# 128-key chunks with a shared tail, stacked scores and per-pair key sums in a fused attention and two-MLP kernel

## Chip, cores and metric

The kernel runs on one core of a Trainium2 chip. The metric is the device time of one execution in microseconds (us). Times of a whole execution are medians over runs. The trace is that of one profiled execution of the kernel before; its times count from the start of the span that the profiler recorded.

## What is computed

Soft-capped attention over 4 batches, 12 heads, 448 positions and 64 features per head, followed by two MLPs over the 1792 tokens (768 features, 2048 hidden).

```python
scores = (q @ k.T) / sqrt(64)
scores = cap * tanh(scores / cap)
attn = exp(scores - max) / (sum(exp(scores - max)) + 1e-09)
x = (attn @ v).transpose(0, 2, 1, 3).reshape(1792, 768)
h = relu(x @ w_in)
x = (h * h) @ moe_w_out
h = x @ moe2_w_in
out = (h / (1 + exp(-1.702 * h))) @ moe2_w_out
```

The weights of the MLPs come as 64-bit floats and are unpacked to 32 bits on the chip.

## The kernel before

With the cap of this input (30) only `bounded_cap` does work; the other version of the kernel, `any_cap`, stands in a branch that is not taken.

**Precision.** Most products are sums of rounded parts: an operand is split into `hi` (rounded to the fp32r type by ScalarE) and `lo` (the rest, by VectorE), and TensorE multiplies the parts and adds them up in PSUM. The attention of batches 0 and 1 (`PLAIN`) multiplies exp(scores) by V as plain fp32 instead; each such product appears as two matmul records. One matmul has 448 moving columns nearly everywhere.

**Attention.** Heads are worked in pairs, 6 pairs per batch; a pair's two heads lie in partitions 0 to 63 and 64 to 127 of the tiles of q and k. Scores are made transposed, keys on partitions: the 448 keys are cut into 4 chunks of 112 (`CP`, `NCH`). For one chunk `scores` issues 6 matmuls: three terms (hi·hi, hi·lo, lo·hi), each for both heads, with 64 rows of the array for each head. `tanhs` and `exps` (ScalarE) then work on 112 partitions and 2 x 448 columns, and `pv` multiplies by V for each head (in batches 2 and 3 once for the hi part of exp and once for the lo part). V's tile has 128 columns per head: in batches 0 and 1 the values and a block of ones, so that the sums over keys come out in the other half of the same matmul; in batches 2 and 3 the hi and the lo part of V.

**Sums of batches 2 and 3.** `add_keys` adds up the chunks of exp on VectorE, `sum_keys` multiplies the split result by a column of ones into 12 partitions of PSUM (one row for each head of the batch), and `take_sums` (VectorE) collects them. Only after the sixth pair of the batch `recip` takes the reciprocals, in four pieces of 112 columns, and splits them; `normalize` spreads them over partitions by matmuls against `spread` (2 for each pair, hi and lo) and multiplies. Batches 0 and 1 use `divide` for each pair instead: a reciprocal of `ct` [128 x 448] (in one piece in batch 0, in four pieces of 112 columns in batch 1), then the product.

**Order.** Work is issued in quarter slots T. Pair n of the 24 begins at `begin[n]` = 8n, plus 14 (`LATE`) from batch 1 on; `PREP`, `PLAN0` (batches 0 and 1) and `PLAN` (2 and 3) say which step goes at which slot after that. Batch 0 runs alone up to slot 52. Then come the four stages of the MLPs, one for each batch, with 68 weight units each; a unit is 15 or 18 matmuls (`product`), and behind each unit `attn` issues as many slots of the next batch's attention as `ready` asks for: in stage 1 (batch 1 in the MLPs, batch 2 in attention) 58 slots, in stage 2 48. A scheduler at build time orders the instructions of each engine from this. Engines take their instructions in order.

**Queues.** SyncE (SP) issues the loads of q, k, v and of the weights (`Q_LOAD`, `Q_V`), GpSimd (POOL) the stores of the first three stages (`Q_OUT`). q and k of batch 0 are transposed by TensorE (`kps`, `qps`), those of the later batches by VectorE.

Of the kernel before, what the change touches and what calls it, by code (L numbers as in the profile page):

```python
# [677 lines left out]
def bounded_cap(ctx, tc, q, k, v, cap, w1, w2, w3, w4, out):  # L678
# [26 lines left out]
    NCH = S // CP  # L705
# [7 lines left out]
    Q_KEEP = nc.sync  # L713

# [7 lines left out]
    LATE = 14  # L722
# [8 lines left out]
    OB = 2  # L731

# [31 lines left out]
    one = const.tile([P, 2 * P], F32R, name="one")  # L764

    spread = [const.tile([P, 2, D], F32R, name=f"spread{i}") for i in range(NP)]
    sums = const.tile([P, S], F32, name="sums")
    rcp = const.tile([P, 2, S], F32R, name="rcp")

    def emit_const():  # L770
        nc.sync.dma_start(out=capt, in_=cap.rearrange("(o n) -> o n", o=1).to_broadcast([P, 1]))
# [10 lines left out]
        nc.gpsimd.memset(f32(one[:, P - 1 : P]), 1.0)  # L782
        nc.gpsimd.memset(f32(rcp), 0.0)

    def emit_spread():
        for i, s in enumerate(spread):
            nc.vector.tensor_copy(s, ident[:, 2 * i : 2 * i + 2].unsqueeze(2).to_broadcast([P, 2, D]))
# [4 lines left out]

    def load_pair(b, p):
        if b in DVE_QK:

            qt = ld.tile([P, S // 32, 32], F32, tag="q", name="qt")
            kt = ld.tile([P, S // 32, 32], F32, tag="k", name="kt")
            for t, src in ((kt, k), (qt, q)):
                for j in range(4):
                    Q_LOAD.dma_start(  # L800
                        out=t[32 * j : 32 * j + 32],
                        in_=src[b, 2 * p + j // 2, :, 32 * (j % 2) : 32 * (j % 2) + 32].rearrange(
                            "(c p) d -> p c d", p=32
                        ),
                    )
        else:
            qt = ld.tile([CP, NCH, 2, D], F32, tag="q", name="qt")
            kt = ld.tile([CP, NCH, 2, D], F32, tag="k", name="kt")
            for t, src in ((kt, k), (qt, q)):
                for j in range(2):  # L810
                    Q_LOAD.dma_start(
                        out=t[:, :, j, :], in_=src[b, 2 * p + j].rearrange("(p c) d -> p c d", c=NCH)
                    )
        raw[b, p] = (qt, kt)

    def transposed(b, t, name):

        if b in DVE_QK:
            y = ld.tile([P, S], F32, tag="tt", name=name)
            nc.vector.transpose(y, t.rearrange("p c d -> p (c d)"))  # L820
            return y
        ps = ps_x.tile([P, 512], F32, tag="x" if name == "kps" else "z", name=name)
        for c in range(NCH):
            cols = slice(c, S, NCH) if name == "qps" else slice(c * CP, (c + 1) * CP)
            nc.tensor.transpose(ps[:, cols], t[:, c].rearrange("p h d -> p (h d)"), ident[:CP, :CP])  # L825
        return ps[:, :S]

    def load_v(b, p):
        if b in PLAIN:

            vt = vst[b, p] = v_p.tile([CP, NCH, 4, D], F32, tag="v", name="vt")
            nc.gpsimd.memset(vt[:, :, 1:3, :], 1.0)
            for j in range(2):
                Q_V.dma_start(
                    out=vt[:, :, 3 * j, :],
                    in_=v[b, 2 * p + j].rearrange(
                        "(c p) d -> p c d" if b in DVE_QK else "(p c) d -> p c d", c=NCH
                    ),
                )
            return  # L840
        vt = v_p.tile([CP, NCH, 2, D], F32, tag="vraw", name="vraw")
        for j in range(2):
            Q_V.dma_start(out=vt[:, :, j, :], in_=v[b, 2 * p + j].rearrange("(c p) d -> p c d", c=NCH))
        vst[b, p] = vt

    def split_v(b, p, half):

        if half == 0:
            t = vst[b, p]
            vs = v_p.tile([CP, NCH, 4, D], F32R, tag="v", name="vs")  # L850
            vst[b, p] = (t, vs)
            nc.scalar.activation(vs[:, :, 0::3, :], t, AF.Copy)
        else:
            t, vs = vst[b, p]
            nc.vector.tensor_tensor(vs[:, :, 1:3, :], t, f32(vs[:, :, 0::3, :]), ALU.subtract)
            vst[b, p] = vs

    def prep_k(b, p, step):
# [531 lines left out]
```

## Time and profile before

| what | us |
|---|---|
| median of 3 runs | 1204.43 |
| lowest, highest run | 1200.18, 1208.26 |
| profiled execution, its own time | 1205.74 |
| its span in the trace | 1203.9 |
| TensorE busy in the span | 1180.6 |
| VectorE busy | 782.1 |
| ScalarE busy | 746.0 |

The span is what lies between the first and the last recorded instruction. PE is TensorE's matmuls, PEld its weight loads, DVE VectorE, ACT ScalarE, POOL GpSimd, SPq the queue of SyncE. The granted TensorE clock is 1.00 of its full 2.4 GHz level in every stretch before the last. Matmuls overlap each other, so the duration of one matmul is not its cost; the distance from one start to the next is. The stages lie as follows: batch 0's attention alone from 0 to 82 us, MLPs of batch 0 with attention of batch 1 to about 390 us, MLPs of batch 1 with attention of batch 2 to about 676 us, then two more, and the last stage without attention.

### The profile page before, as it was taken

To read this page: it belongs to the slowest core of one execution; us is meant where nothing else is said; L and a number is where in the kernel's file an instruction comes from. 1 tells how busy PE (TensorE), PEld (TensorE's weight loads), DVE (VectorE), ACT (ScalarE), POOL (GpSimd) and SP (SyncE) were. 2 spreads that over 40 slices of the span, in tenths; PEclk is the share of its full clock that TensorE was granted. 3 is DMA by queue.
4 is the path that set the end of the run, shared out by engine and by line. 5 is a ranking of instruction groups with operands and counts; after the bars stand their busy time and mean duration, and the time that the engine had idled before them with its cause. 6 is when DMAs were issued, how large, how long until landed. Compare 5 with 4: busy or idle time off the path is not lost.

```text
span 1203.9 us, 15272 instructions
## 1 busy us (share of the span) xinstructions
PE 1180.6 (98%) x5688; PEld 993.8 (83%) x5688; DVE 782.1 (65%) x1078; ACT 746.0 (62%) x1071; POOL 54.5 (5%) x95
## 2 busy tenths in 40 slices
PE   7989999999999999999999999999999999999997
PEld 3448877777777888888888888888899999999996
DVE  2578476776769947787677965676646753564454
ACT  5989677877679647676667575666643444344431
POOL 1000000000001300000000400000000310000000
PEclk9999999999999999999999999999999999999999
DMA  4469877888787753443333432223323432333323
GB/s 107 104 175 321 247 223 233 258 269 230 223 242 240 211 141 93 115 121 102 90 112 108 123 115 78 96 70 105 101 71 118 136 121 94 116 114 111 100 98 50
DMA packets 193223, 174.03 MB, mean 145 GB/s; under 512 B 116466, under 2 KB 165618, under 8 KB 193138
## 3 DMA queue, kind: packets, MB, share of 16 engines
q1 hardware_dynamic: 185266, 168.13, 46.8%
q0 software_dynamic: 2304, 4.13, 1.7%
q10 hardware_dynamic: 5568, 0.69, 0.4%
q8 instruction: 47, 0.77, 0.3%
q14 instruction: 38, 0.31, 0.1%
HBM read 142.25 MB, written 30.67 MB: 144 GB/s over the span
## 4 chain that ended last, share of the span: by engine, by line
PE 92%; ACT 4%; DMA 2%; DVE 1%; issue 1%; SPq 0%; DVEq 0%; ACTq 0%
PE mps L1205 76%; PE vps L935 8%; PE sps L892 6%; DMA wraw<-in_moe_w_in_dram 1%; PE sums L983 1%; ACT e L903 1%; DMA keep<-y 1%; ACT ct L951 1%; ACT wh L1185 1%; ACT e L899 1%; ACT sx L1161 0%; PE rps L1016 0%; DVE y L1168 0%; PE qps L825 0%; DMA qt<-in_q_dram 0%
## 5 line engine op out<-in xcount | busy, mean ns | idle before, releaser
L1205 PE MATMUL mps<-xt,wh 128*128 128x448 f32 x1536 | 444.7, 371 | 4.1 <-ACT xt L1030 1.8
L1205 PE MATMUL mps<-g,wh 128*128 128x448 f32 x1536 | 443.7, 370 | 1.0 <-ACT wh L1185 0.6
L1185 ACT ACTIVATE wh<-wraw 128x768 fp32r<-128x768 f32 (+1 forms) x204 | 164.5, 807 | 275.1 <-PE mps L1205 261.4
L1205 PEld LDWEIGHTS mps<-xt,wh 128*128 128x128 f32 x1536 | 286.1, 188 | 41.3 <-issue 7.6
L1205 PEld LDWEIGHTS mps<-g,wh 128*128 128x128 f32 x1536 | 286.1, 188 | 38.0 <-ACT wh L1185 5.1
L1186 DVE TENSOR_TENSOR wl<-wraw,wh 128x768 fp32r<-128x768 f32 (+1 forms) x204 | 185.4, 909 | 175.0 <-ACT wh L1185 172.8
L1205 PE MATMUL mps<-g,wl 128*128 128x448 f32 x768 | 281.8, 367 | 1.0 <-DVE wl L1186 1.0
L1205 PE MATMUL mps<-xt,wl 128*128 128x448 f32 x768 | 281.4, 366 | 0.0
L1205 PEld LDWEIGHTS mps<-g,wl 128*128 128x128 f32 x768 | 144.3, 188 | 14.6 <-DVE wl L1186 1.9
L1205 PEld LDWEIGHTS mps<-xt,wl 128*128 128x128 f32 x768 | 144.3, 188 | 13.0 <-DVE wl L1186 0.4
L1234 ACT ACTIVATE g<-r 128x448 fp32r<-128x448 f32 x128 | 73.5, 574 | 62.3 <-DVE r L1230 33.2
L1235 DVE TENSOR_TENSOR g<-r,g 128x448 fp32r<-128x448 f32 x128 | 79.4, 621 | 45.4 <-ACT g L1234 44.8
L899 ACT ACTIVATE e<-sps 112x896 f32<-112x896 f32 x96 | 87.4, 911 | 23.0 <-PE sps L892 22.9
L903 ACT ACTIVATE e<-e,ecap 112x896 f32<-112x896 f32 x96 | 99.7, 1039 | 1.8
L1247 DVE SCALAR_TENSOR_TENSOR y<-mps,y 128x448 f32<-128x448 f32 x96 | 59.4, 619 | 57.4 <-PE mps L1205 56.8
L1186 DVE TENSOR_TENSOR wl<-y,wh 128x768 fp32r<-128x768 f32 (+1 forms) x68 | 61.9, 910 | 50.3 <-ACT wh L1185 49.5
L892 PE MATMUL sps<-qq,kk 64*112 64x448 f32 x576 | 90.0, 404 | 1.0 <-ACT qq L878 0.7
L935 PE MATMUL vps<-e,vt 112*128 112x448 f32 x192 | 85.9, 564 | 1.4 <-ACT e L903 0.4
L892 PEld LDWEIGHTS sps<-qq,kk 64*112 64x112 f32 x576 | 45.3, 175 | 46.5 <-issue 27.8
L1263 POOL DMA_DIRECT2D out_dram<-o x72 | 45.2, 635 | 648.5 <-DVE o L1261 648.0
L1161 ACT ACTIVATE sx<-wraw 128x768 f16<-128x768 bf16 (+1 forms) x68 | 69.4, 1021 | 7.0 <-DMA wraw<-in_moe_w_in_dram 5.8
L1168 DVE SCALAR_TENSOR_TENSOR y<-wraw,sx 128x768 int32<-128x768 int32 (+1 forms) x68 | 61.6, 906 | 10.3 <-ACT sx L1161 8.7
(74 smaller groups left out, 887.0 us busy)
## 6 DMA issues: line engine op xcount, KB each, us to landing
wraw<-keep SPq DMA_DIRECT2D x66, 768.0 KB, 4.3
wraw<-in_moe_w_in_dram SPq DMA_DIRECT2D x32, 766.5 KB, 6.4
wraw<-keep SPq DMA_DIRECT2D x36, 640.0 KB, 4.3
keep<-y SPq DMA_DIRECT2D x44, 384.0 KB, 3.4
wraw<-in_moe_w_out_dram SPq DMA_DIRECT2D x24, 638.8 KB, 5.8
wraw<-in_moe_w_out_dram SPq DMA_DIRECT2D x12, 766.5 KB, 6.6
keep<-y SPq DMA_DIRECT2D x24, 320.0 KB, 3.9
kt<-in_k_dram SPq DMA_DIRECT2D x72, 56.0 KB, 4.9
```

The costliest lines, as they stand in the source:

```text
L892: nc.tensor.matmul(ps[:CP, j, :S], kk[r, ik, c * CP : (c + 1) * CP], qq[r, iq, :], start=(i == 0), stop=(i == 2),)
L899: nc.scalar.activation(e, sc.pop((b, p, c))[:CP, :, :S], AF.Tanh)
L903: nc.scalar.activation(e, e, AF.Exp, scale=ecap[:CP])
L935: nc.tensor.matmul(pvp[b, p][j][:, :S], x, t[:, j, :], start=(c == 0 and n == 0), stop=(c == NCH - 1 and n == len(ts) - 1),)
L1161: pin(nc.scalar.activation(z, words(n, BF16)[:, :, :, 2], AF.Copy))
L1168: pin(nc.vector.scalar_tensor_tensor(y[:, :kn].bitcast(I32), words(n, I32)[:, :, :, 0], 13, sx[n % XZ][:, :kn], ALU.logical_shift_right, A ...
L1185: pin(nc.scalar.activation(hi[:, :kn], t[:, :kn], AF.Copy))
L1186: pin(nc.vector.tensor_tensor(lo[:, :kn], t[:, :kn], f32(hi[:, :kn]), ALU.subtract))
L1205: nc.tensor.matmul(ps[:, :S], a[:, kk, :], r, start=(kk == 0 and i == 0), stop=(kk == kn - 1 and i == 2),)
L1234: nc.scalar.activation(g[:, 0, :], r, AF.Copy)
L1235: nc.vector.tensor_tensor(g[:, 1, :], r, f32(g[:, 0, :]), ALU.subtract)
L1247: nc.vector.scalar_tensor_tensor(y, ps[:, :S], scale, y, ALU.mult, ALU.add)
```

## The change

- **Chunks.** In batches 0, 2 and 3 the 448 keys of a head are cut into 3 chunks of 128 and a rest of 64. The rests of the two heads of a pair share one chunk: k lies in a tile of 512 columns per pair (`kz`), head a's 448 keys in columns 64 to 511, head b's first 384 in columns 128 to 511 and its last 64 in columns 0 to 63, with zeros beside the tail's keys in the other head's rows. The tail's scores are then one product over 128 rows, and `tanhs`, `exps`, `split_hi` and `split_lo` work on 448 columns there instead of 896. In `pv` the tail is two products over 64 rows. Batch 1 (`NATURAL`) keeps chunks of 112.
- **Stacked scores in batches 2 and 3.** For each head the 128 rows of the array hold q's hi part and its lo part; k's hi part and lo part are held twice, once in each half of the partitions. A chunk is 4 matmuls over 128 rows (2 for each head) instead of 6 over 64. The copy into the other half is made by two DMAs for each pair from the POOL queue (`Q_DUP`, step 3 of `prep_k`, five slots ahead of the pair's first scores). The ACT and DVE steps of `prep_k` and `prep_q` become two instructions of 64 partitions each.
- **Sums per pair.** `sum_keys` writes each head's sums on 64 partitions; `take_sums` (now on ACT) copies them to `ct`, and batches 2 and 3 use `divide` for each pair, as batch 1 does. `recip`, `normalize`, `spread`, `sums` and `rcp` are gone.
- **Order.** Batches 2 and 3 begin 12 quarter slots later (26 instead of 14). `ready` of batches 2 and 3 becomes 6 slots later, so stage 1 has 64 slots instead of 58; stage 2 stays at 48.

```diff
-    NCH = S // CP
+    NCH = 4
+    TAIL = NCH - 1
+    KW = NCH * P
+    STACKED = (2, 3)
+    NATURAL = (1,)
...
+    Q_DUP = nc.gpsimd
...
-    LATE = 14
+    LATE = (0, 14, 26, 26)
...
+    kz = [const.tile([P, KW], F32, name=f"kz{i}") for i in range(2)]
...
+        nc.vector.memset(kz[0][:32], 0.0)
+        nc.gpsimd.memset(kz[1][:32], 0.0)
...
+            Q_LOAD.dma_start(out=kt[16:, :, 0, :], in_=ka)
+            Q_LOAD.dma_start(out=kt[32:, :, 1, :], in_=kb[:96])
+            Q_LOAD.dma_start(out=kt[:16, :, 1, :], in_=kb[96:])
+            Q_LOAD.dma_start(out=qt[:, :, 0, :], in_=qa)
+            Q_LOAD.dma_start(out=qt[:, :, 1, :], in_=qb)
...
+        Q_V.dma_start(out=ta, in_=va[64:].rearrange("(c p) d -> p c d", p=P))
+        Q_V.dma_start(out=tb, in_=vb[: TAIL * P].rearrange("(c p) d -> p c d", p=P))
+        Q_V.dma_start(out=ca, in_=va[:64])
+        Q_V.dma_start(out=cb, in_=vb[TAIL * P :])
...
+        elif stacked:
+            kk = prep[b, p][1]
+            for j, r, o in halves():
+                Q_DUP.dma_start(out=f32(kk[o, j]), in_=f32(kk[r, j]))
...
+        tail = c == TAIL and b not in NATURAL
...
+        if b in STACKED:
+            todo = [(0 if tail else j, kk[:, j, i, cols], qq[:, j, :]) for j in range(2) for i in range(2)]
+        elif tail:
+            todo = [(0, kk[:, ik, cols], qq[:, iq, :]) for ik, iq in ((0, 0), (0, 1), (1, 0))]
...
+    def chunk(b, c, t):
+        if b in NATURAL:
+            return t[:CP]
+        return t[:, : 1 if c == TAIL else 2]
...
+        if c == TAIL:
+            for j, r, o in halves():
+                nc.vector.tensor_tensor(a[o, j, :], a[o, j, :], e[o, 0, :], ALU.add)
...
+        elif c == TAIL:
+            todo = [(j, vt[o, 2 * TAIL], t[o, 0, :]) for t in ts for j, r, o in halves()]
+        else:
+            todo = [(j, vt[:, 2 * c + j], t[:, j, :]) for j in range(2) for t in ts]
...
-            w = one[:CP, P - 1 - 2 * p - j : 2 * P - 1 - 2 * p - j]
+            w = one[:, D * (1 - j) : D * (1 - j) + P]
...
     def take_sums(b, p):
-        r = slice(0, H)
-        ps = sps.pop((b, p))[:, 0]
-        if p == 0:
-            nc.vector.tensor_copy(sums[r], ps[r, :S])
-        else:
-            nc.vector.tensor_tensor(sums[r], ps[r, :S], sums[r], ALU.add)
-
-    def recip(b, p, step):
...
-    def normalize(b, p, k):
...
+        nc.scalar.activation(pvp[b, p][2], sps.pop((b, p))[:, 0, :S], AF.Copy)
...
-        -5: [(prep_q, 0)],
+        -5: [(prep_q, 0), (prep_k, 3)],
...
-        **{15 + i: [(recip, i)] for i in range(NCH + 1)},
-        **{20 + i: [(normalize, 2 * i)] for i in range(NP // 2)},
+        **{15 + i: [(divide, i)] for i in range(NCH + 1)},
...
-    begin = [8 * n + (LATE if b else 0) for n, (b, p) in enumerate(pairs)]
+    begin = [8 * n + LATE[b] for n, (b, p) in enumerate(pairs)]
```

On TensorE, in batch 0's attention at the end of a pair, the order before is (`sps` scores, `vps` products with V, `kps` and `qps` transposes of k and q):

```order
L892 MATMUL sps<-qq,kk 112x448 x6
L935 MATMUL vps<-e,vt 128x448 x2
L892 MATMUL sps<-qq,kk 112x448 x6
L825 MATMUL kps<-ident,kt 128x112 x4
L935 MATMUL vps<-e,vt 128x448 x2
L892 MATMUL sps<-qq,kk 112x448 x6
```

and now:

```order
L968 MATMUL sps<-qq,kk 128x448 x3
L1028 MATMUL vps<-e,vt 128x448 x2
L968 MATMUL sps<-qq,kk 128x448 x6
L846 MATMUL kps<-ident,kz_120 128x128 x4
L1028 MATMUL vps<-e,vt 128x448 x2
L968 MATMUL sps<-qq,kk 128x448 x6
```

The places stay the same; the tail's scores are 3 matmuls, and the transposes of k have 128 columns.

On VectorE, in stage 1 at the end of a pair of batch 2, the order before is (`x` the pair's result, `sums` its sums, `wl` the lo part of a weight unit, `plo` and `acc` the lo part of exp and the sum of its chunks):

```order
L955 TENSOR_TENSOR x_5248<-vps,ct 64x448 x2
L914 TENSOR_TENSOR plo<-e,phi 112x896
L855 TENSOR_TENSOR vs<-vraw,vs 112x4x128
L1186 TENSOR_TENSOR wl<-wraw,wh 128x768 x2
L924 TENSOR_TENSOR acc<-acc,e 112x896
L1186 TENSOR_TENSOR wl<-wraw,wh 128x768
L993 TENSOR_TENSOR sums<-sums 12x448
```

and now, in another pair's end (`g` is the lo part of an MLP's hidden unit, `r` its activation, `kk` the lo part of k):

```order
L1059 RECIPROCAL ct<-ct 128x112 x4
L1284 SCALAR_TENSOR_TENSOR r<-r,mps 128x448
L1240 TENSOR_TENSOR wl<-wraw,wh 128x768
L1008 TENSOR_TENSOR acc<-acc,e 64x448
L1289 TENSOR_TENSOR g<-r,g 128x448
L996 TENSOR_TENSOR plo<-e,phi 128x448
L1008 TENSOR_TENSOR acc<-acc,e 64x448
L910 TENSOR_TENSOR kk<-kps,kk 64x512
```

The pair now has its own four reciprocals in the queue that also carries `r`, `g` and `wl` of the MLPs; here all four stand together, ahead of an MLP's activation, and the step on `sums` is gone.

## Rows read from the trace of the kernel before

**Rows 1.** The page's first part: busy us, share of the span, instructions of each engine.
```profile
PE 1180.6 (98%) x5688; PEld 993.8 (83%) x5688; DVE 782.1 (65%) x1078; ACT 746.0 (62%) x1071; POOL 54.5 (5%) x95
```
**Rows 2.** Windows: stretch, its length, PE, PEld, DVE, ACT, POOL busy, clock, DMA.
```profile
30.00:60.00 30.00, 29.52 (x130) 13.99 (x128) 16.69 (x20) 27.54 (x35) 1.57 (x3) 1.00 0.46 105
350.00:400.00 50.00, 48.26 (x231) 38.56 (x231) 46.29 (x67) 45.30 (x63) 7.64 (x12) 1.00 0.78 219
500.00:550.00 50.00, 50.00 (x253) 43.20 (x252) 39.02 (x55) 34.88 (x50) 0.00 (x0) 1.00 0.39 111
550.00:600.00 50.00, 50.00 (x253) 43.41 (x252) 33.52 (x45) 35.60 (x52) 0.00 (x0) 1.00 0.33 94
```
**Rows 3.** Timeline of PE in stage 1: start, us, engine, line, operation, count.
```profile
551.32 0.57 PE L1205 MATMUL mps<-xt,wh 128*128 128x448 f32 x2
551.72 0.37 PE L1205 MATMUL mps<-xt,wl 128*128 128x448 f32 x1
552.02 0.87 PE L892 MATMUL sps<-qq,kk 64*112 64x448 f32 x6
552.82 0.68 PE L1205 MATMUL mps<-xt,wh 128*128 128x448 f32 x2
...
556.64 0.37 PE L935 MATMUL vps<-phi,vs 112*128 112x448 f32 x1
556.85 0.37 PE L935 MATMUL vps<-plo,vs 112*128 112x448 f32 x1
```
**Rows 4.** Groups by line and shape: count, busy us, mean ns, idle before.
```profile
L1016 PE MATMUL rps<-rcp,spread 128*128 128x448 f32 x24 | 7.1, 379 | 0.5 <-DVE x L1024 0.4
L967 DVE RECIPROCAL ct<-ct 128x112 f32<-128x112 f32 x24 | 18.7, 820 | 0.1
L869 DVE TENSOR_TENSOR kk<-kps,kk 128x448 fp32r<-128x448 f32 x24 | 14.9, 619 | 24.6 <-ACT kk L866 24.6
L914 DVE TENSOR_TENSOR plo<-e,phi 112x896 fp32r<-112x896 f32 x48 | 51.9, 1082 | 1.3 <-ACT phi L910 1.1
L899 ACT ACTIVATE e<-sps 112x896 f32<-112x896 f32 x96 | 87.4, 911 | 23.0 <-PE sps L892 22.9
```
**Rows 5.** Timeline of PE in batch 0's attention, a pair's end, and the next one's.
```profile
33.77 0.87 PE L892 MATMUL sps<-qq,kk 64*112 64x448 f32 x6
34.56 0.60 PE L825 MATMUL kps<-ident,kt 112*128 112x112 f32 x4
35.00 1.68 PE L935 MATMUL vps<-e,vt 112*128 112x448 f32 x4
...
43.33 1.77 PE L935 MATMUL vps<-e,vt 112*128 112x448 f32 x4
45.03 0.86 PE L892 MATMUL sps<-qq,kk 64*112 64x448 f32 x6
45.83 0.60 PE L825 MATMUL kps<-ident,kt 112*128 112x112 f32 x4
```
**Rows 6.** Timeline of all engines at the start: first loads, first transposes.
```profile
1.57 1.40 SPq L811 DMA_DIRECT2D kt<-in_k_dram  x2
5.20 0.98 PE L825 MATMUL kps<-ident,kt 112*128 112x112 f32 x4 [5.20 <-DMA kt<-in_k_dram]
```
**Rows 7.** Waits of PE from 200 to 400 us: who, for whom, us, times, longest.
```profile
PE mps L1205 <- ACT wh L1185: 0.6, 1, 0.6
PE vps L935 <- DVE plo L914: 0.5, 1, 0.5
...
PE sps L892 <- ACT e L899: 0.3, 1, 0.3
```
**Rows 8.** DMA issues: count, KB each, median us from issue to landing.
```profile
keep<-y SPq DMA_DIRECT2D x44, 384.0 KB, 3.4
out_dram<-o POOLq DMA_DIRECT2D x72, 56.0 KB, 3.2
```

More of the change, by code (lines that the diff above doesn't have):

```diff
@@ L762, in bounded_cap @@
     qs = const.tile([P, 1], F32, name="qs")
[L764 to L768, printed above, removed]
+    one = const.tile([P, 3 * D], F32R, name="one")
+    kz = [const.tile([P, KW], F32, name=f"kz{i}") for i in range(2)]
     def emit_const():
+        nc.vector.memset(kz[0][:32], 0.0)
+        nc.gpsimd.memset(kz[1][:32], 0.0)
         nc.sync.dma_start(out=capt, in_=cap.rearrange("(o n) -> o n", o=1).to_broadcast([P, 1]))
@@ L781, in emit_const, with halves @@
         nc.gpsimd.memset(f32(one), 0.0)
[L782 to L787, printed above, removed]
+        nc.gpsimd.memset(f32(one[:, D : 2 * D]), 1.0)
     pairs = [(b, p) for b in range(B) for p in range(NP)]
     raw, vst, prep, pps, sc, et, hl, acc, pvp, sps, x32, xt = ({} for _ in range(12))
+    def halves():
+        for j in range(2):
+            yield j, slice(64 * j, 64 * j + 64), slice(64 * (1 - j), 64 * (1 - j) + 64)
@@ L806, in load_pair @@
         else:
+            kt = kt.rearrange("p (c h d) -> p c h d", h=2, d=D)
             qt = ld.tile([CP, NCH, 2, D], F32, tag="q", name="qt")
[L808 to L813, printed above, removed]
+            ka, kb, qa, qb = (
+                src[b, 2 * p + j].rearrange("(p c) d -> p c d", c=NCH) for src in (k, q) for j in range(2)
+            )
@@ L823, in transposed @@
         for c in range(NCH):
[L824 to L826 removed]
+            nc.tensor.transpose(
+                ps[:, c:n:NCH], t[:, c].rearrange("p h d -> p (h d)"), ident[: n // NCH, : n // NCH]
+            )
+        return ps[:, :n]
     def load_v(b, p):
[L829 to L840 removed]
@@ L841, in load_v @@
[L841 to L844, printed above, removed]
+        va, vb = v[b, 2 * p], v[b, 2 * p + 1]
+        if b in NATURAL:
+            vt = vst[b, p] = v_p.tile([CP, NCH, 3, D], F32, tag="v", name="vt")
+            nc.gpsimd.memset(vt[:, :, 1], 1.0)
+            for x, src in ((vt[:, :, 0], va), (vt[:, :, 2], vb)):
+                Q_V.dma_start(out=x, in_=src.rearrange("(c p) d -> p c d", c=NCH))
+            return
@@ L930, in pv @@
             pvp[b, p] = [pool.tile([P, 512], F32, tag=tag, name="vps") for tag in tags]
[L931 to L938 removed]
+        ts = [et[b, p, c]] if b in PLAIN else hl[b, p, c]
+        if b in NATURAL:
+            todo = [
+                (j, vt[:, c, j : j + 2, :], t[:, j, :]) for j in range(2) for t in ts
+            ]
+        elif c == TAIL:
+            todo = [(j, vt[o, 2 * TAIL], t[o, 0, :]) for t in ts for j, r, o in halves()]
+        else:
+            todo = [(j, vt[:, 2 * c + j], t[:, j, :]) for j in range(2) for t in ts]
+        for n, (j, x, t) in enumerate(todo):
+            nc.tensor.matmul(
+                pvp[b, p][j][:, :S], x.rearrange("p a d -> p (a d)"), t,
+                start=c == 0 and all(i[0] != j for i in todo[:n]),
+                stop=c == TAIL and all(i[0] != j for i in todo[n + 1 :]),
+            )
     def take_x(b, p, half):
@@ L945, in take_x @@
         ct = pvp[b, p][2]
-        for j in range(2):
+        for j, r, o in halves():
             ps = pvp[b, p][j]
-            r = slice(64 * j, 64 * j + 64)
-            o = slice(64 * (1 - j), 64 * (1 - j) + 64)
             if half == 0:
```

151 lines of the change are left out of this document (84 added, 67 removed).

## Prediction

> **What bounds the kernel now.** I read the busy times first. TensorE's matmuls cover 98% of the span and the next engine, VectorE, 65% [rows 1]. A busy PE could still be a waiting one, so the second view is the table of windows: in the MLP stages PE is busy for the full 50 us of a window [rows 2], and the list of waits has under 2 us for PE in the 200 us that look worst [rows 7]. The third view, the timeline, says what a matmul costs. Its duration is 0.37 us, but the next one starts 0.20 to 0.21 us behind it (two in 0.40 us at 551.32, 0.21 from 556.64 to 556.85) [rows 3]; I take 0.203 as the pitch of a full matmul of 448 columns. So time goes down by what leaves PE, matmul by matmul, and goes up only where another engine comes late. Two stretches differ: batch 0's attention, where ACT is busy for 27.5 of 30 us beside PE's 29.5 [rows 2], and the change from stage 0 to 1, the only window of the middle with a real loss (48.26 of 50 us), at DVE 46.3 and ACT 45.3 [rows 2].
>
> The sums below are made against the profiled execution's own 1205.74 us (span 1203.9); the median of the runs is 1.3 lower, 1204.43, and the predicted time stands on that median.
>
> **Scores of batches 2 and 3.** One chunk now: the matmul ahead of it starts at 551.72, the one behind it at 552.82 [rows 3]. Of these 1.10 us the matmul ahead takes 0.20, so the chunk costs 0.90 us for 6 half-array matmuls. Three full pitches would be 0.61; some 0.29 is lost when PE changes to half-array matmuls and back. After the change a chunk is 4 full matmuls, 4 x 0.203 = 0.81 us, and so is the tail, for the chunk count stays at four. 12 pairs x 4 chunks x 0.085 = **-4.1 us**. With a pitch of 0.20 it is -4.8, with 0.21 it is -2.9.
>
> The Trainium skill speaks against this edit: "TensorE: Matmul & The Clock Gate", Part 3 (Packing small matmuls), gives matmuls on different row groups the span of one plus about 4 ns for each further one. By that rule the old chunk would be an estimated 0.62 us, and the four full matmuls a loss. The row says 0.90, and I go by the row.
>
> **Tail of the product with V, batches 2 and 3.** Four full matmuls for a quarter of the keys (0.81 us) become four half-array ones, hi of both heads, then lo of both. If neighbours run side by side as in the scores, that is two pitches and one change, 0.41 + 0.29 = 0.70: 12 x -0.11 = **-1.4 us**. No row shows two products with V side by side. Lower end, no cost of the change: 0.41, -4.9 us. Upper end, no overlap and the cost of the change: 1.10, +3.5 us. I take the value nearest to the scores' row, which has the same mixture of row groups.
>
> **The spreading of reciprocals goes.** 24 matmuls `rps` [rows 4] x 0.203 = 4.9 us, and the 0.4 us that PE waits there for the multiplication goes too: **-5.3 us**. Their columns are like those of any full matmul, so there is little to bound. The four matmuls of `sums` per pair stay.
>
> **Batch 0's attention.** A pair takes 45.83 - 34.56 = 11.27 us [rows 5]. On PE the pair's tail changes three things. Scores: 34.56 - 33.77 = 0.79 us becomes 3 x 0.203 = 0.61, -0.18. Product with V: both heads' fp32 products take 45.03 - 43.33 = 1.70 us in four records of 0.425. On 64 rows each, and in the order head a, head a, head b, head b, only the second and the third can lie side by side: 1.27, -0.43. Transposes of k: 0.44 us x 128/112, +0.06. Together -0.55 per pair. ACT must allow it: it is busy for 27.5/30 of 11.27, 10.3 us, and loses half of one tanh (0.911 [rows 4]) and half of one exp, taken as long, so 9.4 of the 10.7 us that are left. Six pairs: -3.3 us. Against that the first pair's q stands behind three loads of k in SP's queue instead of two. Two issues took 1.40 us, and PE's first work waits for such a load [rows 6]; one more costs +0.7. The two memsets of `kz` stand ahead of these loads, but the first load is issued at 1.57 us, behind two small ones, and I cost them at nothing. Sum **-2.6 us**. Ends: all of the fp32 tail side by side (0.85 instead of 1.70) -5.1; no overlap and 0.3 us for the change, +1.8.
>
> **Twelve slots later.** Batch 2's first pair leaves the end of stage 0, where DVE and ACT were both over 90% busy and PE lost 1.74 us [rows 2]. The waits there are for hi and lo parts of exp, which only batch 2 and later have, and for a weight's hi part [rows 7]. I take **-1.0 us**, between -1.7 (all of it) and 0 (ACT's weights and batch 1 alone keep it).
>
> **What is added to VectorE.** Per pair: four reciprocals of 0.82 us, 3.3; a second instruction for k and for q, since 64 partitions take as long as 128 (0.62 each by the row of `kk`), 1.2; two additions of 448 columns in the tail for one of 896, +0.2 [rows 4]. Less: half of a `plo`, 0.54; the addition to `sums`, about 0.6; the eight old reciprocals, 0.5 per pair. Net about +3 us per pair, 36 us in all. In stage 1 (some 286 us) a pair comes every 8 of 58 slots, 39 us, and of 64 slots, 35 us. DVE's 36 of 50 us [rows 2] is 28.6 us per pair now: some 15 for attention (eight instructions of 1.08 and ten of about 0.62), 13.6 for the MLPs. After: 18 + 12 = 30 of 35 us, 86%. At 78% (500 to 550 us) PE lost nothing, at 93% it lost 1.74 in 50 us [rows 2]. 86% is between; I take **+1.7 us** for the stage, with 0 and five such windows, +8.7, as ends. What is late first would be `wl` and `g` of the MLPs, queued behind four reciprocals in a row (3.3 us); units of 15 or 18 matmuls (3.0 to 3.7 us) lie ahead of their use. ACT gets one copy and two halves per pair more and three half tails less, which is nearly even.
>
> **The copies of k.** Two DMAs per pair of 256 KB from POOL's queue. The trace has none like it. A 384 KB transfer landed in 3.4 us, a 56 KB one from POOL's queue in 3.2 [rows 8]. They are issued five slots ahead of the first scores, about 22 us in stage 1, and the stores that share the queue come only at the end of a stage. Cost nothing; upper end, both at the rate of the 56 KB row (17.5 KB/us), 29 us, 7.3 us late for each of 12 pairs, +88. The nearest row in size is the 384 KB one, so I take 0; nothing here can fall below it, since the copies replace no transfer.
>
> **Sum.** -4.1 - 1.4 - 5.3 - 2.6 - 1.0 + 1.7 = -12.7 us: 1193.0 on the profiled execution's own time, **1191.7 us** on the median.
>
> **Rivals.**
> - *VectorE takes back half.* With five windows like 350 to 400 us the term is +8.7 instead of +1.7: 1198.7 us. For it: 86% on average is uneven, and a unit's chain runs through ACT and DVE in turn. Against: at 78% nothing showed, and there are two units of lead.
> - *Half-array products of fp32 overlap fully, DVE costs nothing.* Batch 0 gives -5.1 and the last term 0: 1187.5 us. For it: 64-row scores do lie side by side [rows 3]. Against: the records come in order, head by head.
> - *The loss of 0.29 us belongs to the scores, not to the half arrays.* Then a stacked chunk pays 0.81 + 0.29 = 1.10: +9.6 instead of -4.1, 1205.4 us, no gain. Against it: the products with V, whose operands change as well, start 0.21 us apart without such a gap [rows 3]. The Trainium skill's rule of Part 3 (Packing small matmuls, same page) would make this term an estimated +9 from the other end, a cheaper old chunk, which the row of 0.90 us does not bear out.
> - *The copies come late (the other side).* The place is the first scores of each pair of batches 2 and 3: PE takes its instructions in order, so all MLP matmuls queue behind a pair's scores. It decides from 22 us between issue and landing; from 23.2 us on, 1.2 us late in each of 12 pairs, the gain is gone and the kernel is slower, and at the 29 us above it ends near 1280 us. Against it: both rows of 3 us.
>
> **How the numbers follow.** Chances: forecast 0.50, VectorE 0.24, full overlap 0.18, scores keep their loss 0.04, copies late 0.04. Within the forecast the ends of the terms give about 1187 to 1196. A measurement of this kernel can tell about 1% (12 us) from no change, so faster means under 1192.4: six tenths of the forecast (0.30), all of the full overlap (0.18) and a little of the rest, 0.50. Same: the other four tenths, VectorE, and the lost scores, 0.46. Slower: late copies, 0.04. The range that leaves 2 in 10 out reaches from 1185, half of the further gain of the V tail beyond the full overlap's time, to 1200, just past VectorE's case.
>
> **What would show it.** Right: PE's records of `sps` in batches 2 and 3 in groups of four, the next matmul 1.0 us behind the one ahead of the group instead of 1.10; `vps` of a tail in 0.7 us; no `rps`; batch 0's pairs every 10.7 us and the first MLP matmul near 79 us instead of 82; PE full in all windows of stage 1 with DVE at 80 to 88%. Wrong: waits of PE for `wl`, `g` or `plo` of several us in stage 1, waits of `sps` for the DMA of `kk`, or gaps around the groups of four.

## The result, and the profile after

The changed kernel takes 1186.59 us (median of 4 runs, 1183.74 to 1188.05) against 1204.42 us of the kernel before in the same job. The ratio is 0.985, 95% interval 0.981 to 0.989, so some 17.8 us are gone. The same kernel was run once more later and gave 1185.64 us, ratio 0.9852 [0.9829, 0.9874]. The profiled execution took 1188.05 us, its span is 1185.9 us.

The first part of the page, which answers to [rows 1]:

```profile
PE 1156.4 (98%) x5550; PEld 998.9 (84%) x5550; DVE 818.0 (69%) x1135; ACT 749.9 (63%) x1105; POOL 67.4 (6%) x139
```

PE has 24 us less and VectorE 36 us more (818.0 - 782.1), as the prediction added up. The windows, as the first three of [rows 2]:

```profile
30.00:60.00 30.00, 26.60 (x121) 13.95 (x121) 16.89 (x19) 25.91 (x36) 2.27 (x12) 1.00 0.47 112
350.00:400.00 50.00, 49.43 (x238) 44.09 (x237) 48.43 (x73) 36.05 (x57) 16.15 (x26) 1.00 0.83 226
500.00:550.00 50.00, 49.83 (x243) 44.65 (x242) 46.64 (x68) 38.52 (x58) 2.05 (x4) 1.00 0.50 131
```

Two things stand out. In batch 0 (30 to 60 us) PE is busy for 26.6 us instead of 29.5, and yet the stretch is hardly shorter, as will be seen. In stage 1 VectorE reaches 93% of a window (46.64 of 50 us; over the whole stage it is 83%) and PE stays full but for 0.17 us.

PE's timeline in stage 1, as in [rows 3] (start, us, engine, line, operation): one chunk of scores, and one tail of the product with V.

```profile
574.51 0.36 PE L1259 MATMUL mps<-g,wl 128*128 128x448 f32 x1
574.71 0.97 PE L968 MATMUL sps<-qq,kk 128*128 128x448 f32 x4
575.52 0.56 PE L1259 MATMUL mps<-g,wh 128*128 128x448 f32 x2
...
587.89 0.36 PE L1259 MATMUL mps<-xt,wl 128*128 128x448 f32 x1
588.18 0.47 PE L1028 MATMUL vps<-phi,vs 64*128 64x448 f32 x2
588.48 0.36 PE L1028 MATMUL vps<-plo,vs 64*128 64x448 f32 x2
588.77 0.67 PE L1259 MATMUL mps<-xt,wh 128*128 128x448 f32 x2
```

From the matmul ahead of the chunk to the one behind it are 1.01 us (575.52 - 574.51); less one pitch that is 0.81 us for the chunk. The tail costs 588.77 - 587.89 - 0.20 = 0.68 us: products with V on half the rows do lie side by side in pairs.

The reciprocals by line and shape, as in [rows 4] (72 where there were 24), and the issues of the copies of k, as in [rows 8]:

```profile
L1059 DVE RECIPROCAL ct<-ct 128x112 f32<-128x112 f32 x72 | 56.7, 824 | 0.1
```

```profile
kk<-kk POOLq DMA_DIRECT2D x24, 256.0 KB, 3.0
```

There is no `rps` any more, and no wait of PE for a copy of k: they land 3.0 us after their issue (median; the longest takes 5.2). The list of PE's waits (engine, line, waited for: us in total, times, longest) from 200 to 400 us, which answers to [rows 7], and from 400 to 700 us:

```profile
PE mps L1259 <- ACT wh L1239: 0.6, 2, 0.4
PE mps L1259 <- DVE wl L1240: 0.2, 1, 0.2
```

```profile
PE mps L1259 <- ACT g L1288: 0.2, 1, 0.2
```

Batch 0's attention, PE's timeline as in [rows 5]; the last row is the first matmul of the MLPs:

```profile
32.47 0.65 PE L846 MATMUL kps<-ident,kz 128*128 128x128 f32 x4
33.06 1.02 PE L1028 MATMUL vps<-e,vt 64*128 64x448 f32 x4
33.57 1.12 PE L968 MATMUL sps<-qq,kk 64*128 64x448 f32 x6
...
35.68 0.99 PE L1028 MATMUL vps<-e,vt 128*128 128x448 f32 x2 [1.00 <-ACT e L985]
...
43.59 0.66 PE L846 MATMUL kps<-ident,kz 128*128 128x128 f32 x4
...
79.23 0.68 PE L1259 MATMUL mps<-xt,wh 128*128 128x448 f32 x2 [2.71 <-DVE x L1045]
```

A pair takes 43.59 - 32.47 = 11.12 us, not 10.7: what PE saved it spends waiting for ACT's exp, 1.00 us in each pair.

Where the time went, by the timelines of the two profiles: the first MLP matmul comes 2.75 us earlier (81.98 and 79.23 us), stage 0 is 10.85 us shorter, stage 1 2.4, stage 2 1.5, and stage 3, which has no attention at all, 2.35. (Stages 1 to 3 begin at 398.9, 686.2 and 958.6 us before and at 385.3, 670.2 and 941.1 us now; the 390 and 676 us given for the kernel before are some 10 us too early.) Stages 0 and 1 have to be read together, for the later start moves work from the one to the other: in the run below that changes nothing else, stage 0 is 14.7 us shorter and stage 1 11.1 us longer. The last matmul ends up 19.9 us earlier, and 1.9 us of that are lost again behind it. Two of these entries cannot come from the change: stage 3, and, as the experiments show, the start.

### The profile page after: what moved, and what is told of

Same layout as the page of the kernel before. It is cut to its first block, busy times and chain, and to the rows that moved or that the text cites. A ratio compares the mean times of both kernels' runs of the same rounds, so it can differ in the third digit from the quotient of the medians.

```text
span 1185.9 us, 15305 instructions
## 1 busy us (share of the span) xinstructions
PE 1156.4 (98%) x5550; PEld 998.9 (84%) x5550; DVE 818.0 (69%) x1135; ACT 749.9 (63%) x1105; POOL 67.4 (6%) x139
## 4 chain that ended last, share of the span: by engine, by line
PE 93%; ACT 3%; DMA 2%; DVE 1%; issue 1%; SPq 0%; DVEq 0%; ACTq 0%
PE mps L1259 77%; PE vps L1028 8%; PE sps L968 6%; DMA wraw<-in_moe_w_out_dram 1%; PE sums L1075 1%; ACT e L985 1%; ACT e L981 0%; ACT wh L1239 0%; PE kps L846 0%; DVE wl L1240 0%; ACT ct L1043 0%; DMA qt<-in_q_dram 0%; PE qps L846 0%; DVE y L1222 0%; ACT sx L1215 0%
## 5 line engine op out<-in xcount | busy, mean ns | idle before, releaser
L1259 PEld LDWEIGHTS mps<-xt,wl 128*128 128x128 f32 x768 | 144.2, 188 | 13.4 <-issue 0.9
L968 PE MATMUL sps<-qq,kk 128*128 128x448 f32 (+2 forms) x462 | 95.1, 399 | 0.7 <-ACT qq L930 0.7
L985 ACT ACTIVATE e<-e,ecap 128x896 f32<-128x896 f32 (+1 forms) x96 | 93.0, 970 | 1.8
L981 ACT ACTIVATE e<-sps 128x896 f32<-128x896 f32 (+1 forms) x96 | 80.6, 841 | 18.7 <-PE sps L968 18.6
L1028 PE MATMUL vps<-e,vt 112*128 112x448 f32 (+2 forms) x192 | 79.6, 555 | 6.1 <-ACT e L985 5.2
L968 PEld LDWEIGHTS sps<-qq,kk 128*128 128x128 f32 (+2 forms) x462 | 60.8, 185 | 27.1 <-issue 20.0
L1239 ACT ACTIVATE wh<-y 128x768 fp32r<-128x768 f32 (+1 forms) x68 | 54.6, 803 | 22.4 <-DVE y L1222 12.6
```

Source lines behind the costliest of these rows:

```text
L968: nc.tensor.matmul(ps[:m, u, :S], x, y, start=all(t[0] != u for t in todo[:n]), stop=all(t[0] != u for t in todo[n + 1 :]),)
L981: nc.scalar.activation(e, chunk(b, c, sc.pop((b, p, c)))[:, :, :S], AF.Tanh)
L985: nc.scalar.activation(e, e, AF.Exp, scale=ecap[:CP] if b in NATURAL else ecap)
L1028: nc.tensor.matmul(pvp[b, p][j][:, :S], x.rearrange("p a d -> p (a d)"), t, start=c == 0 and all(i[0] != j for i in todo[:n]), stop=c == T ...
L1239: pin(nc.scalar.activation(hi[:, :kn], t[:, :kn], AF.Copy))
L1259: nc.tensor.matmul(ps[:, :S], a[:, kk, :], r, start=(kk == 0 and i == 0), stop=(kk == kn - 1 and i == 2),)
```

## The experiments

The questions: what the later start of batches 2 and 3 is worth, which of the parts of the attention pays, why batch 0 gained nothing, and whether VectorE has room left. To compare profiles I use the time from the first to the last MLP matmul, which leaves the start out:

| kernel | first MLP matmul | last | between | median us |
|---|---|---|---|---|
| before | 81.98 | 1195.77 | 1113.8 | 1204.4 |
| before, again | 79.41 | 1189.58 | 1110.2 | 1199.99 (one run) |
| before, later start | 81.86 | 1189.78 | 1107.9 | 1199.6 |
| sums per pair, start at 14 | 79.56 | 1190.04 | 1110.5 | 1203.4 |
| sums per pair, start at 26 | 79.58 | 1182.69 | 1103.1 | 1195.7 |
| unstacked | 81.46 | 1178.38 | 1096.9 | 1188.0 |
| changed | 79.23 | 1175.91 | 1096.7 | 1186.6 |
| changed, again | 79.27 | 1173.81 | 1094.5 | 1185.6 |
| batch 0 in 112-key chunks | 79.78 | 1174.41 | 1094.6 | 1185.9 |
| changed, start at 14 | 80.09 | 1185.63 | 1105.5 | 1197.5 |
| changed, start at 20 | 79.67 | 1186.69 | 1107.0 | 1195.8 |
| changed, start at 34 | 80.03 | 1177.38 | 1097.4 | 1187.4 |

Two profiles of one kernel differ by 2 to 4 us in the fourth column, so smaller differences there mean nothing.

**The later start, taken out of the changed kernel.**

```diff
-    LATE = (0, 14, 26, 26)
+    LATE = (0, 14, 14, 14)
```

> The changed kernel with all batches from 1 on at 14 slots again, as before the change. Theory A (the later start): the changed kernel gained some 7 us between 200 and 410 us, where batch 2's first pair used to be worked in clumps beside the weights' unpacking of stage 0; with the old start these clumps come back, 5 to 7 us slower than the changed kernel's 1186.6 us, so 1191.6 to 1193.6 and a ratio to before near 0.990. Theory B (the smaller attention work itself makes the clumps vanish): within 1 us of 1186.6, ratio 0.985.

Measured: 1197.53 us, ratio to before 0.996 [0.9949, 0.9971]. Against the changed kernel (0.9852) that is 0.0108, 13 us, about twice what theory A expected: nearly three quarters of the whole gain hang on this one line. The place shows in the windows of the end of stage 0 and in PE's timeline there:

```profile
367.00:371.00 4.00, 4.00 (x22) 3.18 (x21) 3.94 (x8) 2.66 (x5) 0.00 (x1) 1.00 1.01 349
371.00:376.00 5.00, 1.85 (x7) 1.36 (x7) 3.86 (x6) 4.93 (x7) 1.02 (x2) 0.79 0.49 108
376.00:384.00 8.00, 6.91 (x17) 4.62 (x16) 7.78 (x11) 7.25 (x11) 0.00 (x0) 0.50 0.74 243
```

```profile
370.79 1.08 PE L968 MATMUL sps<-qq,kk 128*128 128x448 f32 x4
375.02 0.74 PE L1075 MATMUL sums<-phi,one 128*128 128x448 f32 x1 [3.15 <-ACT e L981]
```

Near the end of the stage batch 2's chunks stand one behind the other, with no MLP matmuls between them that could hide tanh, exp and the two splits. PE stands still for 3.15 us, until a tanh (L981) is done, and ACT is busy for 4.93 of 5 us; meanwhile the granted clock falls to 0.50, the 1.2 GHz level, and from 376 to 384 us PE does 17 matmuls where 367 to 371 had 22 in 4. Between 360 and 395 us PE's waits come to 4.2 us (0.6 us in the changed kernel), and the clock is at 0.50 for some 10 us, in 8 of which PE is busy; at half the clock that is 4 us more. So an estimated 8 of the 13 us lie in this one place. It is not a chance of one profile: the mean granted clock is 0.991 to 0.994 in all eleven runs, and 0.996 to 0.998 in the nine of the changed kernel.

**The later start alone, in the kernel before.**

```diff
-    LATE = 14
+    LATE = (0, 14, 26, 26)
...
-    begin = [8 * n + (LATE if b else 0) for n, (b, p) in enumerate(pairs)]
+    begin = [8 * n + LATE[b] for n, (b, p) in enumerate(pairs)]
```

> The kernel before with nothing but the later start of batches 2 and 3 (26 slots instead of 14). Theory A (the later start): the clumps at the end of stage 0 go, 5 to 7 us faster than before, 1197.4 to 1199.4 us, ratio 0.994 to 0.996. Theory B (the smaller work): 1204 us, ratio 1.000 within its interval.

Measured: 1199.59 us, ratio 0.9963 [0.995, 0.9977], a gain of 4.5 us (2.8 to 6.0), a little under the 5 to 7 of theory A. What the prediction had overlooked stands in stretches in which PE is "busy" all the time. The window 260 to 360 us, of before and of this run:

```profile
260.00:360.00 100.00, 100.00 (x456) 77.64 (x455) 68.42 (x93) 73.57 (x101) 0.53 (x1) 1.00 0.80 238
```

```profile
260.00:360.00 100.00, 100.00 (x464) 80.68 (x463) 72.79 (x99) 75.77 (x104) 0.53 (x1) 1.00 0.88 275
```

By the groups of the two stretches both hold 40 matmuls of the product with V; before has 62 of the scores and 354 of the MLPs, this run 50 and 374. Twelve half-array matmuls at 0.15 us (0.89 / 6) are 1.8 us, twenty full ones at 0.205 are 4.1: before does 2.3 us less work in the same 100 us, without a wait. Its timeline shows how, first one product with V between MLP matmuls, then two that stand between scores:

```profile
154.55 1.67 PE L935 MATMUL vps<-e,vt 112*128 112x448 f32 x4
155.70 0.92 PE L1205 MATMUL mps<-xt,wh 128*128 128x448 f32 x2
...
326.32 1.67 PE L935 MATMUL vps<-e,vt 112*128 112x448 f32 x4
327.92 0.86 PE L892 MATMUL sps<-qq,kk 64*112 64x448 f32 x6
328.71 1.77 PE L935 MATMUL vps<-e,vt 112*128 112x448 f32 x4
330.41 0.87 PE L892 MATMUL sps<-qq,kk 64*112 64x448 f32 x6
```

The same four fp32 matmuls cost 1.15 us (155.70 - 154.55) in front of full matmuls and 1.60 to 1.70 in front of half-array scores. In all of batch 1's attention 8 of the 24 products with V stand whole in front of half-array scores before, and 3 in this run, where MLP matmuls stand between the steps again: 5 x 0.5 = 2.5 us. By the rows it is the half arrays that make the difference, not the scores as such. With the start at 14 in the changed kernel, two of these products stand in front of stacked scores, which use the full array, and cost 1.26 us at 331.12 and 1.15 us here:

```profile
333.75 1.67 PE L1028 MATMUL vps<-e,vt 112*128 112x448 f32 x4
334.90 1.33 PE L968 MATMUL sps<-qq,kk 128*128 128x448 f32 x4
```

The changed kernel has not got rid of this loss: 7 of its 24 still stand in front of half-array scores (11 with the start at 14), some 3.5 us.

**Other starts.**

```diff
-    LATE = (0, 14, 26, 26)
+    LATE = (0, 14, 20, 20)
```

> The changed kernel with batches 2 and 3 at 20 quarter slots instead of 26. Theory that what counts is how much of batch 2's first pair runs before the end of stage 0: 1188 to 1193 us, between 1185.6 at 26 and 1197.5 at 14. Rival, only the order that the scheduler happens to find decides: any time from 1184 to 1198, without order in the series.

```diff
-    LATE = (0, 14, 26, 26)
+    LATE = (0, 14, 34, 34)
```

> The changed kernel with batches 2 and 3 at 34 quarter slots. Theory that at 26 the end of stage 0 is already free of batch 2: 1184 to 1187 us, no gain that can be measured. Rival, what PE still loses in stage 0 is batch 2's doing: 1180 to 1183 us.

Measured: at 20 slots 1195.8 us, ratio 0.9946 [0.9925, 0.9967]; at 34 slots 1187.36 us, ratio 0.988 [0.986, 0.99]. With 14 (0.996) and 26 (0.9852) the series goes down in order and is flat behind 26, but not evenly: nearly all of it falls between 20 and 26. At 20 slots the same picture lies a little later, and is nearly as dear (waits of 1.61 and 2.57 us, and a granted clock of 0.50 from 393.5 to 400 us):

```profile
392.97 0.47 PE L1075 MATMUL sums<-phi,one 128*128 128x448 f32 x1 [1.61 <-ACT phi L992]
396.01 0.74 PE L1028 MATMUL vps<-phi,vs 128*128 128x448 f32 x1 [2.57 <-DVE x L1047]
```

So 1195.8 lies above the 1188 to 1193 expected. The rival is not excluded: 1195.8 lies in its range, and four starts of which two have the bunch and two have not could come from the order that the scheduler finds. That 26 is late enough is borne out by 34.

**Sums per pair, with and without the later start.** Batches 1 to 3 in 112-key chunks, unstacked; of the change there remain the sums per pair, the start and batch 0.

```diff
-    STACKED = (2, 3)
+    STACKED = ()
...
-    NATURAL = (1,)
+    NATURAL = (1, 2, 3)
```

(`load_v`, `split_v`, `pv` and `sum_keys` follow with tiles of 112 partitions.)

> Batches 1, 2 and 3 in 112-key chunks with unstacked scores; what is left of the change in batches 2 and 3 is the sums per pair and the start 12 slots later. Theory of unit costs: against the changed kernel 48 score chunks at 0.89 instead of 0.82 us (+3.3) and 12 tails of the V product at 0.82 instead of 0.70 (+1.5), so 1190 to 1193 us. Rival, the reciprocals of each pair on VectorE take back what the 24 spreading matmuls cost: the time stays at that of the kernel before with the later start alone, 1198 to 1200 us.

Measured: 1195.68 us, ratio 0.9925 [0.9906, 0.9944]. Against the later start alone (0.9963) that is -4.6 us, and by the table -4.8 (1103.1 and 1107.9), batch 0's change included: the 24 matmuls `rps`, forecast at 5.3 us, are gone, and the reciprocals do not take that back. The run came out 3 us above the range expected.

> The kernel of e6_sums_per_pair, but batches 2 and 3 begin at 14 quarter slots instead of 26. Theory that the sums per pair and the start at 14 get in each other's way (four reciprocals per pair on VectorE in the crowded end of stage 0): 7 to 13 us more than e6_sums_per_pair, 1200 to 1206 us. Rival, the two add up as they do in the kernel before (4 us for the start): 1197 to 1200 us.

(The same with `LATE = (0, 14, 14, 14)`.) Measured: 1203.4 us, ratio 1.0004 [0.999, 1.0018]. So the sums per pair gain 4.6 us at 26 slots and nothing at 14; put the other way, the later start is worth 4.5 us in the kernel before (1 - 0.9963) and 9.5 us here (1.0004 - 0.9925). The two get in each other's way, by as much as the first theory had it. The timeline shows the same sign as above, here a wait for a weight's hi part, and two matmuls of 1.11 us together behind it, twice their usual 0.57, at a granted clock of 0.50 (373 to 379.5 us):

```profile
373.77 1.11 PE L1266 MATMUL mps<-xt,wh 128*128 128x448 f32 x2 [1.87 <-ACT wh L1246]
```

But the reason that this theory gave is not seen there. In this profile no reciprocal runs on VectorE between 347 and 402 us, and what PE waits for comes from ACT. What the place costs can be estimated: 2.2 us of waits from 360 to 395 us, 2.9 us for the 5.7 us that PE works at half the clock, and 3.4 us for 14 products with V in front of half-array scores where the run with the start at 26 has 7. That is 8.5 of the 9.5 us. Which part of the sums per pair brings the steps together there stays open.

**Unstacked scores.**

```diff
-    STACKED = (2, 3)
+    STACKED = ()
```

> The changed kernel with batches 2 and 3 not stacked: chunks of 128 keys and the shared tail stay, scores are again 6 half-array matmuls for a full chunk and 3 full ones for the tail, no copies of k. Theory A (TensorE's unit costs decide): 36 full chunks at 0.892 instead of 0.824 us, +2.4 us; 12 tails at 3 x 0.205 instead of 0.824, -2.5 us; together 0, so 1186.6 within 1 us, ratio 0.985. Theory B (stacking is worth the 3 to 4 us that the forecast gave it): 1190 us, ratio 0.988.

Measured: 1187.98 us, ratio 0.9878 [0.9864, 0.9892], 3 us above the changed kernel with overlapping intervals; by the table 1096.9 against 1096.7 and 1094.5. The ratio is theory B's, the unit costs behind theory A are borne out by the rows, and the runs do not decide between the two. A pair here is three chunks of 6 half-array matmuls and a tail of 3 full ones:

```profile
557.02 0.36 PE L1259 MATMUL mps<-xt,wl 128*128 128x448 f32 x1
557.32 0.87 PE L968 MATMUL sps<-qq,kk 64*128 64x448 f32 x6
558.12 0.68 PE L1259 MATMUL mps<-g,wh 128*128 128x448 f32 x2
...
566.94 0.37 PE L1259 MATMUL mps<-g,wl 128*128 128x448 f32 x1
567.14 0.77 PE L968 MATMUL sps<-qq,kk 128*128 128x448 f32 x3
567.75 0.57 PE L1259 MATMUL mps<-g,wh 128*128 128x448 f32 x2
```

That is 3 x (1.10 - 0.20) + (0.81 - 0.20) = 3.31 us for a pair against 4 x 0.81 = 3.24 stacked, 0.8 us over 12 pairs. So by the rows the shared tail brings most of the scores' gain, and stacking 0.8 us; by the ratios stacking brings 3 us, which these runs can tell neither from 0.8 nor from zero. From the run before this one (0.9925) to here, which is the shared tail in the scores and in the product with V, 5.7 us are gained; by the rows 12 x (4 x 0.89 - 3.31) = 3.0 and 12 x (0.82 - 0.68) = 1.7, together 4.7.

The Trainium skill ("TensorE: Matmul & The Clock Gate", Part 3 (Packing small matmuls)) would give the half-array chunk an estimated 0.62 us and so make this kernel 12 x 3 x 0.28 = some 10 us faster than it is. The 0.90 us of its rows, which include changing to half arrays and back, do not agree with that.

**Batch 0 in chunks of 112.**

```diff
-    NATURAL = (1,)
+    NATURAL = (0, 1)
```

(and the loads of k and q on 112 partitions.)

> The changed kernel with batch 0 in chunks of 112 keys again, as batch 1. Theory A (batch 0's part is worth what the start of the first MLP matmul shows): that start goes back from 79.2 to 82.0 us, 2.7 us slower, 1189.3 us, ratio 0.9875. Theory B (the pairs are held by ScalarE's chain at the pair's end, 11.1 against 11.25 us per pair, and the rest is the start): 1 us slower, 1187.6 us, ratio 0.986.

Measured: 1185.93 us, ratio 0.9862 [0.9843, 0.9881], as theory B has it and the same as the changed kernel within what can be measured. Batch 0's new chunks are worth nothing that shows. They may even cost something later: here 3 of batch 1's 24 products with V stand in front of half-array scores, in the changed kernel 7, and stage 0 takes 304.8 us here against 306.1 and 306.7. The first MLP matmul came at 79.78 us, early as in the changed kernel, so the 2.75 us at the start had to have another source. The kernel before was profiled once more:

> The kernel before once more, for a second profile of its start. If TensorE's step from twice the duration of a matmul to the full rate comes by chance before or after the first product with V, this profile may show the first vps group of four at 1.7 to 1.8 us instead of 3.35, the third pair's kps at 21 us instead of 23.3 and the first MLP matmul near 80 us instead of 82. If the changed batch 0 brings the early step, it shows 3.35 us again.

Measured: the first MLP matmul at 79.41 us. One row each of the first profile of before and of the second:

```profile
14.12 3.35 PE L935 MATMUL vps<-e,vt 112*128 112x448 f32 x4
```

```profile
13.56 1.74 PE L935 MATMUL vps<-e,vt 112*128 112x448 f32 x4 [0.31 <-issue]
```

The same four matmuls take 3.35 us in the one and 1.74 in the other. TensorE's step to the full rate comes ahead of them or behind them, in the same kernel; before, before with the later start, unstacked and doubled reciprocals show the late step in their profiles, the others the early one. Early against early, batch 0's change brings 79.41 - 79.23 = 0.2 us, late against late (81.98 and 81.46) 0.5.

**Exp ahead of the copy of k, in batch 0.**

```diff
+        ins = nc.scalar.activation(e, e, AF.Exp, scale=ecap[:CP] if b in NATURAL else ecap)
+        if b == 0 and c == 0:
+            first_exp[:] = [ins.ins]
...
+                with ExitStack() as behind:
+                    if b == 0 and first_exp:
+                        behind.enter_context(tc.issue_after(first_exp[0]))
+                    nc.scalar.activation(kk[:, 0, :], ps, AF.Copy)
```

(and step 1 and 2 of `prep_k` one slot later in `PLAN0`.)

> In batch 0 the copy of k on ACT is put behind the exp of the pair's first chunk (and behind the two copies to ct) instead of ahead of it. Theory that this copy on ACT is what PE's 1.00 us per pair waits for: exp ends 0.6 to 1.1 us earlier, a pair takes 10.1 to 10.5 us instead of 11.12, and the kernel gains 3 to 5 us (1181 to 1184). Rival, the banks of the V product are freed too late by VectorE's copy to x, which comes next: under 1 us.

Measured: 1186.56 us, ratio 0.9847 [0.9826, 0.9869], no gain. (One of the six runs took 6490.66 us and is not in the ratio; why is not known.) ACT, VectorE and PE in one pair:

```profile
34.30 1.04 ACT L988 ACTIVATE e<-e,ecap 128x896 f32<-128x896 f32 x1
35.37 1.10 ACT L1048 ACTIVATE ct<-vps 64x448 f32<-64x448 f32 x2
```

```profile
35.94 1.28 DVE L1050 COPY x<-vps 64x448 f32<-64x448 f32 x2 [4.07 <-ACT ct L1048]
```

```profile
36.66 1.74 PE L1033 MATMUL vps<-e,vt 128*128 128x448 f32 x4 [1.22 <-POOL vt L868]
```

Exp ends at 35.34 now, but PE's product waits to 36.66. The memset of `vt` that the row names is long done; what ends just ahead is the first of VectorE's two copies to `x` (35.94 plus half of 1.28 is 36.58), which by the kernel's buffers frees the bank that the product writes. A pair takes 10.94 us instead of 11.12. The rival holds: behind the wait for exp stands the next one.

**Reciprocals twice.**

```diff
+            if b > 1:
+                nc.vector.reciprocal(spare, ct[:, cols])
             nc.vector.reciprocal(ct[:, cols], ct[:, cols])
```

> Each of the four reciprocals per pair of batches 1... no: of batches 2 and 3 alone is done twice, the first time into a spare tile: +3.3 us on VectorE per pair, 12 pairs, 40 us in all. Theory that VectorE has room left: its share in stage 1 goes from 88% to about 97% and the time grows by under 1.5 us. Rival, VectorE stands just under the point from which it decides: PE waits for wl, g or plo in stage 1, and the time grows by 4 to 10 us.

Measured: 1186.91 us, ratio 0.9856 [0.9832, 0.988], against 0.9852 of the changed kernel in the same job: 0.5 us, within the interval. The window 500 to 550 us:

```profile
500.00:550.00 50.00, 50.00 (x247) 45.59 (x247) 49.51 (x74) 38.32 (x59) 2.04 (x4) 1.00 0.43 125
```

VectorE is busy for 49.5 of 50 us and PE misses nothing; over all of stage 1 VectorE is busy for 89% instead of 83%, and PE's waits are 0.4 us in all. The theory of room is right.

**The changed kernel again**, for the three runs beside it (1185.64 us, above):

> The changed kernel unaltered, on the chip and in the job of the three runs beside it. Both theories: 1185 to 1188 us.

None of the variants beats the changed kernel by more than its interval.

## Why the prediction was right, and where it was not

The forecast was 1191.7 us, range 1185 to 1200; 1186.6 lies in it, 5 us under the forecast. The gain of 12.7 us was 17.8. Step by step:

- **Scores, -4.1.** The size is right: the next matmul stands 1.01 us behind the one ahead of the chunk, forecast 1.0, before 1.10. In these rows it is 0.81 instead of 0.90, -4.3 us over 48 chunks. But the prediction booked it to stacking. By the rows unstacked scores with the shared tail cost only 0.8 us more, so the rest is the shared tail's; the runs (3 us, intervals overlapping) do not settle the split.
- **Tail of the product with V, -1.4.** 0.68 us where 0.70 was forecast: 12 x (0.68 - 0.81) = -1.6.
- **Reciprocals' spreading, -5.3.** -4.6 by the ratios, -4.8 by the table, both with batch 0's change in it. It holds at 26 slots alone; at 14 the sums per pair bring nothing.
- **Batch 0, -2.6.** This step failed. "ACT must allow it" was worked out from ACT's busy time, 9.4 us of a pair of 10.7. But the chain scores, tanh, copy of k, copy to `ct`, exp, product runs through ACT in one order: its busy sum fits, its place does not. PE waits 1.00 us in each pair and 2.71 instead of 1.56 us ahead of the first MLP matmul. The half-array products of fp32 even overlap fully, as the rival had it: the four of a tail start at 33.06 us and the next scores at 33.57, and these take 1.12 us instead of 0.87, some 0.76 us together where the rival had 0.85. It is worth nothing there. "First MLP matmul near 79" came true for the wrong reason, the early step of TensorE's rate.
- **Twelve slots later, -1.0.** The term that was mis-sized: alone it is -4.5 us. The prediction read stage 0's loss off the busy share, 1.74 us in one window [rows 2]. As much again (2.3 us from 260 to 360 us) lay in stretches where PE was busy all the time, with steps of attention so close that products with V cost 1.60 to 1.70 us instead of 1.15. Moreover, it costed the start apart from the other changes. In place, with the new work, the later start is worth 13 us, an estimated 8 of them waits and half clock in one place that the kernel before does not have. Without it, the changed kernel would have gained about 5 us.
- **Added VectorE work, +1.7.** Nothing of it shows; not even 40 us more do. The 93% with a loss [rows 2] that set the scale was the end of stage 0, where ACT unpacks weights as well; a window of stage 1 at 99% loses nothing. There units of MLP matmuls lie between the chunks; that this is the reason was not tested. (Stage 1 had 55 slots before by the kernel's own plan, not 58, since the last step of `PLAN` stood at slot 22 and now stands at 19; `ready` moves by 9. The prediction's 86% is not changed by it; measured are 83%.)
- **Copies of k, 0.** They land in 3.0 us, and no matmul waits for them.

The terms as measured, -4.3 - 1.6 - 4.6 - 0.2 - 4.5 + 0, make -15.2 us. The ratio's interval reaches from -13.4 to -22.8 us, so what is left need not be anything. In the order in which the runs stand, the ratios give -4.5 for the start, -4.6 for the sums per pair (with batch 0), -5.7 for the shared tail and -3.4 for stacking. That the total came within 5 us is in part luck: all but the start was forecast at -11.7 us and brings -4.8 at the old start (0.996), and the start, forecast at -1.0, makes up for it. Of the rivals, the full overlap with free VectorE work stood nearest in time (1187.5), and both its premises held; but its gain did not come from there. VectorE's taking back half, the scores' keeping their loss and late copies are excluded by the rows above.

What stays open is why the chunks of batch 2 come in one bunch near the end of stage 0 when they start early: the timeline shows that they do, and no run here changed their order with the start kept. Nor is it known why a product with V is dearer in front of half arrays, or why the bunch costs so much more with the new work than in the kernel before.

## What to carry to other kernels

A busy share of 100% is not a full rate: the same matmuls cost 1.15 or 1.60 to 1.70 us by what stands next to them, so compare distances between starts, and counts by shape in stretches of equal length. When a change both alters the work and moves the place where it runs, price the two together, in the stretch where they meet; a test of two by two runs tells the interaction from the parts. And before a saving on the bound engine is booked, follow the chain that feeds it: where that chain sets the pace, the saving turns into a wait.

## What the runs showed that was not expected

- **The step at the start.** With the profile's granted clock at 1.00 all the while, the first matmuls take about twice as long as the same ones later, and when the step comes differs between executions of one kernel (3.35 and 1.74 us for the same four matmuls, above); the first MLP matmul comes some 2.3 us earlier or later for it.
- **The clock behind a wait.** Near the end of stage 0, waits of PE of 1.6 to 3.2 us came with a granted clock of 0.50 for 7 to 10 us (starts at 14 and 20 slots with the new work). Ahead of the first MLP matmul PE waits for 2.71 us in all ten profiles with the new batch 0; in four of them (the changed kernel twice, unstacked, doubled reciprocals) the clock stays at 1.00, in the other six it is at 0.50 for about 3 us behind the wait, an estimated loss of 1.5 us. The run with exp first, over six us:

```profile
78.00:84.00 6.00, 4.54 (x15) 4.11 (x16) 5.91 (x6) 4.44 (x6) 0.00 (x0) 0.72 1.00 349
```

- **Two pitches.** At a granted clock of 1.00 full matmuls start 0.207 us apart in some long stretches and 0.203 in others. The same 80 us of stage 3 hold 388 matmuls in the first profile of the kernel before and 397 in the second:

```profile
1090.00:1170.00 80.00, 80.00 (x388) 72.66 (x388) 36.49 (x50) 31.82 (x50) 0.00 (x0) 1.00 0.32 106
```

```profile
1090.00:1170.00 80.00, 80.00 (x397) 74.13 (x396) 37.26 (x51) 32.18 (x51) 0.00 (x0) 1.00 0.30 99
```

Over 1000 matmuls that is some 4 us, as much as a term of the sum above. It explains the 2.35 us of stage 3, which the change does not touch: in the second profile of before that stage takes 234.8 us, as in the changed kernel.
